# Softmax denominators of five more blocks through turning DMAs and GpSimd, in an attention and maxout kernel on one core

## The chip, the core and the metric

The kernel runs on one core of a Trainium2 chip. The metric is the device time of one execution, in microseconds (us). The core has a matrix engine (TensorE, shown as PE, its weight loads as PEld), a vector engine (VectorE, DVE), an activation engine (ScalarE, ACT), GpSimd (POOL) and SyncE (SP). Each takes its own instructions in a fixed order, and they wait for each other through semaphores. Transfers are issued from SP or from POOL and then run on the core's 16 DMA engines.

## The reference

An induced attention (32 learned points, 4 batches of 12544 rows of 128) is followed by a maxout layer without nonlinearity outside the maximum:

```
def mab(q, kv):
    s = scale * (q @ kv.transpose(0, 2, 1))
    s = s - s.max(-1, keepdims=True)
    a = np.exp(s)
    a /= a.sum(-1, keepdims=True) + 1e-09
    return a @ kv
h = mab(I, x)            # I: the 32 inducing points, for each batch
attn = mab(x, h)         # for each of 50176 rows: a softmax over 32
out = np.maximum(attn @ w1, attn @ w2) @ w_out     # d_ff 1024
```

In the second attention the denominator of a row is the sum of its 32 exponentials. The division by it is put off to the very end: the layer is linear but for the maximum, and a maximum commutes with a positive factor.

## The kernel before

**Tiling.** A batch is 98 chunks of 128 rows. Chunks are grouped into 28 blocks, seven for each batch, mostly 16 chunks in four "quarters" of four. A block's exponentials stand in one tile `e2` of 128 x 512: partition 32q+m holds inducing point m for quarter q, and the columns are rows of x. `stage` computes the scores of a block with four column-tiled matmuls (each uses a quarter of the array's columns) and `stage_exp` takes the exponential on ACT.

**The main loop.** For every block the kernel needs max(h1, h2) = h1 + relu(h2 - h1). A "phase" (`phase`, line 1093 of the profile) is four row-tiled matmuls that run beside each other, one for each quarter, into four PSUM banks. Each result of 128 x 512 is then put through a relu on ACT (line 1119) or DVE (line 1122). Between phases stand the "finals": 128 x 128 matmuls (`final_one`, line 907) that multiply those tiles by w_out into the bank of an output group (up to four chunks). The share of h1 is added by small matmuls of line 1093 with `m` (`L` jobs of a phase). `evict_group` (line 939) multiplies a finished group by the reciprocal of its denominators on DVE, and a DMA (line 969) issued from SP or POOL stores it. Output tiles `o` have six buffers.

**Denominators, first way.** `dens` multiplies each 128 x 128 piece of `e2` by `ones_q` (128 x 4) on TensorE: four sums for each row of x, one 128 x 4 matmul for each chunk column, up to two blocks in one call. Line 698 is the matmul, line 708 the reciprocal on DVE.

**Denominators, second way.** For blocks with `turned` set (the last batch, blocks 21 to 27) TensorE isn't used. `den_turn` issues a DMA that transposes `e2` from SP into a tile `eT` (line 717), `den_sum` adds up the 32 values on GpSimd in five halving additions (lines 727 and 729) in the space of `w1T`, and `den_rp` takes the reciprocal on DVE (line 736). The three are jobs in a list `pending`.

**The other transfers on SP.** x arrives by loads from POOL (line 166). For batches 1 to 3, `transpose_x_dma` turns it into `xT` with 14 transposing DMAs (line 172). `pool_scores` and `pool_turn` then make and turn the exponentials of the first attention (`eT`, line 378), and `pool_accum` sums them into h on TensorE (line 397). `den` and `eT` tiles come from one pool of buffers.

**What sets the order.** Every instruction stands in an order that is found when the program is built. `Clock` keeps an estimate of when TensorE, ACT, DVE and each PSUM bank are free. The loop at the end of the kernel asks it at every step whether to issue a phase, a final, or one of the side jobs for which `ready` says yes. `evict_relu` sends each relu to the engine that the estimate frees first. `DEV` is a table that overrides single decisions.

Of the kernel before, what the change touches and what calls it, by code (L numbers as in the profile page):

```python
# [16 lines left out]
INF = 1e9  # L17


class Clock:  # L20


    PAIR = 0.0558
# [4 lines left out]
    def __init__(self):  # L28
        self.pe = self.act = self.dve = 0.0
        self.mode = "full"  # L30
        self.bank = [0.0] * 8
        self.idle = {}
        self.log = []
        self.busy = {}
# [34 lines left out]
class Block:  # L69


    def __init__(self, quarters, full=()):
        self.quarters = quarters
        self.width = max(qu.w for qu in quarters if qu)
        self.b = [qu.b for qu in quarters if qu][0]
        self.staged = None
        self.rp = None
        self.units = []
        self.done = {}
        self.relu = {}  # L80
        self.last_group = {}
        self.groups = []
        for q, qu in enumerate(quarters):
            jobs = []
            t0 = 0
            for w in qu.subs if qu else []:
                for u in range(2 * w):
                    jobs.append((q, t0, w, u))
                t0 += w
            self.units.append(jobs)  # L90
            if qu:
                self.groups.append(Group(self, [(q, t) for t in range(qu.w)], q in full))
# [10 lines left out]
def kernel(  # L103
# [29 lines left out]
    rpp = ctx.enter_context(tc.tile_pool(name="rpp", bufs=5))  # L133
# [34 lines left out]
    def transpose_x_dma(b, j):  # L168
        i, h = divmod(j, 2)
        k0, n = parts[b][i]  # L170
        m = n // 2
        nc.sync.dma_start_transpose(
            xT_tiles[b % 2][:, k0 + m * h : k0 + m * (h + 1), :], xn_at[b, i][:, m * h : m * (h + 1), :]
        )
        st[b]["T", j] = ck.pe
# [21 lines left out]
    with tc.manual_schedule(engines={ET.PE, ET.DVE, ET.Activation, ET.Pool, ET.SP}):  # L197
# [128 lines left out]
        NEU = 5  # L326
        NU = K // U
# [7 lines left out]
        def pool_scores(b, u):  # L335
# [19 lines left out]
            ck.bank[bi] = ck.on_act(end, 0.65)  # L355
# [20 lines left out]
        def pool_turn(b, u):  # L376
            eT = etp.tile([128, 4, 128], F16, name=f"eT_{b}_{u}", tag="eT", bufs=NEU)
            nc.sync.dma_start_transpose(eT, st[b]["eu", u][0].rearrange("p (j t) -> p j t", j=4))
            st[b]["eT", u] = eT, ck.pe

        def pool_accum(b, u):
# [7 lines left out]
            if last:  # L389
                nc.vector.reduce_sum(out=acc[:, C : C + 1], in_=st[b]["es"], axis=AX.X)  # L390
                ck.on_dve(st[b]["eu", u][1], 0.1)
# [33 lines left out]
            end = ck.run(0.58 if last else 0.49, "col")  # L425
# [190 lines left out]

        for n, blk in enumerate(blocks):
            blk.turned = n > 20

        def stage(blk, now=True):  # L620
# [25 lines left out]
            end = ck.run(0.054 * wd, "col")  # L646
# [36 lines left out]
        def dens(blk):  # L683
# [23 lines left out]
            end = ck.run(0.029 * n)  # L707
            nc.vector.reciprocal(out=rp[:, 0:n, :].rearrange("p t q -> p (t q)"), in_=ps[:, 0 : 4 * n])
            ck.bank[bi] = ck.on_dve(end, 0.18 + 0.001 * 4 * n)
            for blk in blks:  # L710
                blk.rpr = ck.dve + 0.2

        def den_turn(blk):
# [3 lines left out]
            nc.sync.dma_start_transpose(eT, e2.rearrange("p (t k) -> p t k", k=128))  # L717
            blk.den = eT, ck.pe
            pending.append((den_sum, (blk,)))

        def den_sum(blk):
            wd = blk.width
            eT = blk.den[0].rearrange("p t (q m) -> p (t q) m", m=M)
            lo = 512 * (blk.index % 2)
# [5 lines left out]
            blk.dsum = acc[:, :, 0], ck.pe  # L730
            pending.append((den_rp, (blk,)))

        def den_rp(blk):
# [3 lines left out]
            ck.on_dve(ck.pe, 0.066 + 0.025 * wd)  # L737
# [187 lines left out]
        def evict_group(g, end):  # L925
# [40 lines left out]
            for b, c, s, m in runs:  # L966
                h = 2 if m == 4 and not by_pool and (gi in (56, 60, 64, 68, 72, 76) or 78 <= gi < 95) else m
                for lo in range(0, m, h):
                    queue.dma_start(out=outr[b, :, c + lo : c + lo + h, :], in_=osb[:, s + lo : s + lo + h, :])  # L969
# [24 lines left out]
        def want_linear():  # L994
# [113 lines left out]
        def evict_relu(q, a, u, bi, ps, end, eng=None):  # L1108
# [6 lines left out]
            ready = end + 0.03  # L1115
            if eng is None:
                eng = max(ck.act, ready) + 0.477 <= max(ck.dve, ready) + 0.597
            if eng:
                nc.scalar.activation(out=dst, in_=src, func=AF.Relu)  # L1119
                t = ck.on_act(ready, 0.477)  # L1120
            else:
                nc.vector.tensor_scalar(out=dst, in0=src, scalar1=0.0, scalar2=None, op0=ALU.max)  # L1122
                t = ck.on_dve(ready, 0.597)
# [36 lines left out]
        def ready(f, a):  # L1160

            now = ck.pe
            if f is den_turn:
                return a[0].staged <= now
            if f is den_sum:
                return a[0].den[1] + 7.5 <= now
            if f is den_rp:
                return a[0].dsum[1] + 3.0 <= now and a[0].index <= groups[min(state["g"], len(groups) - 1)].blk.index + 1
# [3 lines left out]
            if f is pool_turn and a[1] >= NEU and ("sum", a[1] - NEU) not in d:  # L1172
# [117 lines left out]
        while state["g"] < len(groups) or held:  # L1290
# [4 lines left out]
            if state["phase"] >= 3 and "m1" not in st[0] and w_of["w1out"] <= ck.pe and (ck.mode == "full" or final_ready() >= INF):  # L1295
# [71 lines left out]
```

## Time and profile before

| | |
|---|---|
| three runs | 324.11, 324.15, 324.23 us (median 324.15) |
| the profiled execution | 324.28 us, of which its span is 322.5 us |
| mean granted TensorE clock | 0.994 |
| line 698 on PE | 76 matmuls in 11 calls |
| line 736 on DVE | 7 reciprocals |
| HBM read and written | 27.54 MB and 25.69 MB |

The span runs from the first to the last instruction of the core; the times hold 1.78 us more in the profiled execution. Matmuls are pipelined: each has some 200 ns from its start to its end, while the next starts earlier, so the distance from start to start, not the busy time, says what one costs.

### The profile page before, as it was taken

To read this page: it belongs to the slowest core of one execution; us is meant where nothing else is said; L and a number is where in the kernel's file an instruction comes from. 1 tells how busy PE (TensorE), PEld (TensorE's weight loads), DVE (VectorE), ACT (ScalarE), POOL (GpSimd) and SP (SyncE) were. 2 spreads that over 40 slices of the span, in tenths; PEclk is the share of its full clock that TensorE was granted. 3 is DMA by queue.
4 is the path that set the end of the run, shared out by engine and by line. 5 is a ranking of instruction groups with operands and counts; after the bars stand their busy time and mean duration, and the time that the engine had idled before them with its cause. 6 is when DMAs were issued, how large, how long until landed. Compare 5 with 4: busy or idle time off the path is not lost.

```text
span 322.5 us, 12607 instructions
## 1 busy us (share of the span) xinstructions
PE 316.3 (98%) x5372; PEld 241.3 (75%) x5372; DVE 280.9 (87%) x506; ACT 281.6 (87%) x565; POOL 63.2 (20%) x136
## 2 busy tenths in 40 slices
PE   7999999999999999999999999999999999999996
PEld 3976777777777777777777777777777777777786
DVE  3369999899979998898999998989998999899973
ACT  4779899999978999989888999988969999999960
POOL 7472012212040121221040021222006400330000
PEclk9899999999999999999999999999999999999999
DMA  8999999974289999984269999963525322442233
GB/s 206 207 263 213 218 235 233 228 152 102 100 172 241 219 234 230 239 137 128 101 124 239 232 250 226 242 133 117 118 92 109 132 83 88 120 134 95 88 116 116
DMA packets 74072, 54.12 MB, mean 168 GB/s; under 512 B 56064, under 2 KB 64032, under 8 KB 74016
## 3 DMA queue, kind: packets, MB, share of 16 engines
q1 hardware_dynamic: 64320, 27.88, 40.7%
q0 software_dynamic: 9552, 25.37, 33.5%
q8 instruction: 42, 0.69, 0.9%
q14 instruction: 14, 0.11, 0.1%
q10 hardware_dynamic: 144, 0.07, 0.1%
HBM read 27.54 MB, written 25.69 MB: 165 GB/s over the span
## 4 chain that ended last, share of the span: by engine, by line
PE 92%; DMA 5%; ACT 1%; issue 1%; POOL 0%; DVE 0%; POOLq 0%
PE ps L907 62%; PE ps L1093 23%; DMA xn<-in_x_dram 5%; PE ps L637 2%; PE ps L397 2%; PE ps L341 1%; ACT relu L1119 1%; PE ps L698 1%; PE ps L531 0%; PE ps L236 0%; PE ps L315 0%; PE ps L442 0%; PE ps L266 0%; ACT hwd L504 0%; PE ps L489 0%
## 5 line engine op out<-in xcount | busy, mean ns | idle before, releaser
L1119 ACT ACTIVATE relu<-ps 128x512 f16<-128x512 f32 x462 | 244.0, 605 | 23.6 <-PE ps L1093 16.1
L1122 DVE TENSOR_SCALAR relu<-ps 128x512 f16<-128x512 f32 x322 | 206.5, 682 | 17.7 <-PE ps L1093 15.2
L907 PE MATMUL ps<-woutp,relu 128*128 128x128 f16 x3136 | 216.9, 220 | 0.1
L907 PEld LDWEIGHTS <-relu 128*128 128x128 f16 x3136 | 176.7, 98 | 38.7 <-issue 28.2
L1093 PE MATMUL ps<-e,hwd 32*128 32x512 f16 (+2 forms) x888 | 88.9, 358 | 0.6 <-ACT hwd L504 0.6
L969 POOL DMA_DIRECT2D out_dram<-o x44 | 23.8, 542 | 148.3 <-DVE o L939 134.1
L939 DVE TENSOR_TENSOR o<-ps,rp 128x512 f32<-128x512 f32 (+3 forms) x80 | 51.2, 639 | 1.6 <-PE ps L907 1.1
L1093 PEld LDWEIGHTS <-hwd 32*128 32x128 f16 x888 | 24.9, 91 | 22.1 <-issue 0.9
L1093 PE MATMUL ps<-m,e 32*128 32x128 f16 x381 | 38.9, 217 | 0.0
L1093 PEld LDWEIGHTS <-e 32*128 32x128 f16 x381 | 21.3, 92 | 2.9 <-issue 0.4
L939 DVE TENSOR_TENSOR o<-ps,rpt 128x512 f32<-128x512 f32 (+3 forms) x28 | 17.3, 619 | 4.2 <-PE ps L884 2.2
L166 POOL DMA_DIRECT2D xn<-in_x_dram x33 | 17.9, 556 | 6.4 <-DMA xn<-in_x_dram 4.5
L247 DVE COPY xT<-ps 128x768 f16<-128x768 f16 (+6 forms) x11 | 4.8, 459 | 8.7 <-PE ps L236 8.7
L352 ACT ACTIVATE eu<-ps 128x512 f16<-128x512 f32 x18 | 10.8, 616 | 0.0
L236 PE MATMUL ps<-identity,xn 128*128 128x128 f16 x98 | 9.5, 237 | 1.2 <-DVE inducingT L786 0.6
L656 ACT ACTIVATE e<-ps 128x512 f16<-128x512 f32 (+2 forms) x21 | 10.4, 584 | 0.0
L727 POOL TENSOR_TENSOR w1T<-den 128x256 f32<-128x256 f16 (+1 forms) x7 | 4.4, 630 | 26.7 <-DMA den<-e 26.7
L729 POOL TENSOR_TENSOR w1T<-w1T 128x64 f32<-128x64 f32 (+4 forms) x28 | 8.4, 300 | 2.2
L236 PEld LDWEIGHTS <-xn 128*128 128x128 f16 x98 | 6.7, 106 | 2.8 <-DVE xn L748 0.9
L250 ACT COPY xT<-ps 128x768 f16<-128x768 f16 (+5 forms) x10 | 6.4, 670 | 2.1 <-PE ps L236 2.0
L637 PE MATMUL ps<-xT,hT 128*32 128x512 f16 (+3 forms) x118 | 8.3, 355 | 0.0
L637 PEld LDWEIGHTS <-hT 128*32 128x32 f16 x118 | 3.2, 94 | 3.8 <-issue 2.1
(95 smaller groups left out, 115.1 us busy)
## 6 DMA issues: line engine op xcount, KB each, us to landing
out_dram<-o POOLq DMA_DIRECT2D x44, 256.0 KB, 3.8
xn<-in_x_dram POOLq DMA_DIRECT2D x24, 448.0 KB, 9.7
out_dram<-o SPq DMA_DIRECT2D x28, 256.0 KB, 2.7
out_dram<-o SPq DMA_DIRECT2D x46, 128.0 KB, 1.8
wf<-in_moe_w_dram POOLq DMA_DIRECT2D x4, 256.0 KB, 5.9
xn<-in_x_dram POOLq DMA_DIRECT2D x3, 224.0 KB, 8.8
xT<-xn SPq DMA_TRANSPOSE x42, 5.5
xf<-in_x_dram SPq DMA_DIRECT2D x1, 512.0 KB, 3.7
```

What stands on the lines that cost most here:

```text
L166: nc.gpsimd.dma_start(out=xn_at[b, i][lo:hi, 0:n, :], in_=xr[b, lo:hi, k0 : k0 + n, :])
L236: nc.tensor.transpose(ps[:, j, :], xn_at[0, i][:, g + j, :], identity16)
L352: nc.scalar.activation(out=eu, in_=ps, func=AF.Exp, scale=scale, accum_out=st[b]["es"][:, u : u + 1])
L637: nc.tensor.matmul(out=ps[32 * q : 32 * (q + 1), 128 * t : 128 * (t + n)], lhsT=hq, rhs=xT[:, c : c + n, :], start=True, stop=True, tile_p ...
L656: nc.scalar.activation(out=blk.e2[:, lo:hi], in_=ps[:, lo:hi], func=AF.Exp, scale=st[0]["rs"] if blk.b == 0 else scale,)
L729: nc.gpsimd.tensor_add(acc[:, :, 0:n], acc[:, :, 0:n], acc[:, :, n : 2 * n])
L907: nc.tensor.matmul(out=g.ps[:, 128 * c : 128 * (c + 1)], lhsT=g.blk.relu[q][:, 128 * (jb * w4 + t) : 128 * (jb * w4 + t + 1)], rhs=woutp[: ...
L939: nc.vector.tensor_mul(osb[:, 0:n, :], g.ps[:, 0 : n * C].rearrange("p (s c) -> p s c", s=n), rp)
L969: queue.dma_start(out=outr[b, :, c + lo : c + lo + h, :], in_=osb[:, s + lo : s + lo + h, :])
L1093: nc.tensor.matmul(**seq[i])
L1119: nc.scalar.activation(out=dst, in_=src, func=AF.Relu)
L1122: nc.vector.tensor_scalar(out=dst, in0=src, scalar1=0.0, scalar2=None, op0=ALU.max)
```

## The change

`TURNED` names twelve blocks in place of the last seven: 5, 10, 11, 12 and 19 are new. Their `dens` calls go, and `den_turn`, `den_sum` and `den_rp` come for each. The pool of `eT` has six buffers in place of five, that of the reciprocals nine in place of five. `Clock` gets estimates for SP, for POOL and for the time in which x is being loaded, and several of its costs are set anew. `ready` starts a turning only when no load runs by these estimates. Six more groups and three fewer whole ones are stored in halves, `small_m1(0)` may come one phase earlier, and `DEV` is another table.

```
-    PAIR = 0.0558
+    PAIR = 0.05595
...
+    def on_sp(self, ready, us, slow=0.0):
+        self.sp = max(self.sp, ready)
+        self.sp += slow if slow and self.sp < self.loads else us
+        return self.sp + (8.0 if self.sp < self.loads else 4.0)
...
-    rpp = ctx.enter_context(tc.tile_pool(name="rpp", bufs=5))
+    rpp = ctx.enter_context(tc.tile_pool(name="rpp", bufs=9))
...
+                ck.loads = ck.pe + 26.5
...
+        TURNED = (5, 10, 11, 12, 19, 21, 22, 23, 24, 25, 26, 27)
         for n, blk in enumerate(blocks):
-            blk.turned = n > 20
+            blk.turned = n in TURNED
...
         def den_turn(blk):
             uid[0] += 1
-            eT = etp.tile([128, 4, 128], F16, name=f"den_{uid[0]}", tag="eT", bufs=NEU)[:, 0 : blk.width, :]
+            eT = etp.tile([128, 4, 128], F16, name=f"den_{uid[0]}", tag="eT", bufs=NEU + 1)[:, 0 : blk.width, :]
             e2 = blk.e2[:, 0 : 128 * blk.width]
             nc.sync.dma_start_transpose(eT, e2.rearrange("p (t k) -> p t k", k=128))
-            blk.den = eT, ck.pe
+            eTs.append(lambda: blk.dsum is not None)
+            blk.den = eT, ck.on_sp(ck.pe, 1.3)
+            turned.append(blk)
             pending.append((den_sum, (blk,)))
...
-            lo = 512 * (blk.index % 2)
+            lo = 512 * (turned.index(blk) % 2)
...
-                h = 2 if m == 4 and not by_pool and (gi in (56, 60, 64, 68, 72, 76) or 78 <= gi < 95) else m
+                h = 2 if m == 4 and not by_pool and (70 <= gi < 77 and gi not in (74, 75) or 78 <= gi < 95) else m
...
         DEV = {
-            20000: 2, 50900: 2, 61200: 2, 91300: 1, 101300: 1, 111700: 1, 160800: 1, 210000: 3, 220000: 3,
...
+            20000: 2, 51000: 2, 61100: 2, 101200: 1, 101300: 1, 111700: 1, 141400: 1, 160000: 3, 161200: 1,
...
-                eng = max(ck.act, ready) + 0.477 <= max(ck.dve, ready) + 0.597
+                eng = max(ck.act, ready) + 0.487 <= max(ck.dve, ready_v) + 0.601
...
             if f is den_turn:
-                return a[0].staged <= now
+                if len(eTs) > NEU and not eTs[-NEU - 1]():
+                    return False
+                n = len(turned)
+                return a[0].staged <= now and ck.loads <= now and ck.sp <= now + (8.0 if a[0].b == 2 else 0.8) and (n < 3 or turned[n - 3].dsum is not None)
             if f is den_sum:
-                return a[0].den[1] + 7.5 <= now
+                n = turned.index(a[0])
+                return a[0].den[1] + 3.0 <= now and ck.pool <= now and (n < 2 or turned[n - 2].rp is not None)
             if f is den_rp:
-                return a[0].dsum[1] + 3.0 <= now and a[0].index <= groups[min(state["g"], len(groups) - 1)].blk.index + 1
+                return a[0].dsum[1] + 2.5 <= now
```

Counted over the whole built program, instructions change so: TensorE has 20 pairs of weight load and 128 x 4 matmul fewer (56 in place of 76) and otherwise the same matmuls, with as many changes between row-tiled, column-tiled and whole-array work (472) as before. Eleven relus move from DVE to ACT. DVE has two reciprocals of line 708 fewer and five of line 736 more. GpSimd has 25 additions more. SP issues five transposing DMAs and, through the other splitting, three stores more.

On SP this is the stretch in which the x of batch 2 is turned and its first attention runs; `xT` are the turned x, `eT` the turned exponentials of that attention, `o` the output tiles. Before:

```order
L172 DMA_TRANSPOSE xT_94<-xn_88 128x7x128 x2
L378 DMA_TRANSPOSE eT_0_3174<-eu_0_3130 128x4x128
L172 DMA_TRANSPOSE xT_94<-xn_89 128x7x128 x2
L172 DMA_TRANSPOSE xT_94<-xn_90 128x7x128
L378 DMA_TRANSPOSE eT_1_3361<-eu_1_3312 128x4x128
L172 DMA_TRANSPOSE xT_94<-xn_90 128x7x128
L378 DMA_TRANSPOSE eT_2_3487<-eu_2_3441 128x4x128
L378 DMA_TRANSPOSE eT_3_3517<-eu_3_3455 128x4x128
L378 DMA_TRANSPOSE eT_4_3802<-eu_4_3764 128x4x128
L378 DMA_TRANSPOSE eT_5_3831<-eu_5_3771 128x4x128
L969 DMA out_dram<-o_4012 128x512
```

With the change, `den_3122`, `den_3488` and `den_3593` being blocks 10, 11 and 12:

```order
L731 DMA_TRANSPOSE den_3122<-e_332_2341 128x4x128
L179 DMA_TRANSPOSE xT_94<-xn_88 128x7x128 x2
L387 DMA_TRANSPOSE eT_0_3201<-eu_0_3160 128x4x128
L179 DMA_TRANSPOSE xT_94<-xn_89 128x7x128
L387 DMA_TRANSPOSE eT_1_3255<-eu_1_3188 128x4x128
L179 DMA_TRANSPOSE xT_94<-xn_89 128x7x128
L179 DMA_TRANSPOSE xT_94<-xn_90 128x7x128 x2
L731 DMA_TRANSPOSE den_3488<-e_477_3167 128x4x128
L387 DMA_TRANSPOSE eT_2_3510<-eu_2_3467 128x4x128
L387 DMA_TRANSPOSE eT_3_3522<-eu_3_3474 128x4x128
L731 DMA_TRANSPOSE den_3593<-e_479_3174 128x4x128
L387 DMA_TRANSPOSE eT_4_3693<-eu_4_3665 128x4x128
```

Three of the five new turnings stand here: block 10's ahead of the last six pieces of x, block 11's right behind the last piece, and block 12's between the turnings of the first attention. None is moved past a store, but each `xT` and `eT` behind one of them is issued later by its time on SP.

On GpSimd the same stretch holds nothing but stores before; with the change the sums of blocks 11 and 12 stand between them (`w1T` is the space for the sums):

```order
L990 DMA out_dram<-o_3719 128x512
L743 TENSOR_TENSOR w1T<-den_3488 128x256
L745 TENSOR_TENSOR w1T<-w1T 128x16x8
L745 TENSOR_TENSOR w1T<-w1T 128x16x4
L745 TENSOR_TENSOR w1T<-w1T 128x16x2
L745 TENSOR_TENSOR w1T<-w1T 128x16
L990 DMA out_dram<-o_3786 128x512
L743 TENSOR_TENSOR w1T<-den_3593 128x256
```

The store of `o_3786` now comes after a sum that waits for a turning. Behind the four further additions of block 12 come two more stores and then the loads of x for the last batch.

On DVE the reciprocals of blocks 11 and 12 (`rpt_3928`, `rpt_4010`) come ahead of the output groups that need them:

```order
L440 TENSOR_TENSOR hacc_3626<-ps_3888,hacc_3626 128x128
L753 RECIPROCAL rpt_3928<-w1T 128x16
L1142 TENSOR_SCALAR relu_3688<-ps_3940 128x512
L956 TENSOR_TENSOR o_3965<-ps_3841,rpt_3477 128x512
L1142 TENSOR_SCALAR relu_3952<-ps_3969 128x512
L1142 TENSOR_SCALAR relu_3688<-ps_3998 128x512
L753 RECIPROCAL rpt_4010<-w1T 128x16
L1142 TENSOR_SCALAR relu_3952<-ps_4028 128x512
L1142 TENSOR_SCALAR relu_3746<-ps_4030 128x512
L956 TENSOR_TENSOR o_4041<-ps_3938,rpt_3928 128x512
```

Before, one reciprocal of line 708 for both blocks stood about there, behind a `dens` call on TensorE. Now each stands behind a sum on GpSimd, and the relus and output groups after it wait with it.

More of the change, by code (lines that the diff above doesn't have):

```diff
@@ L29, in __init__ @@
         self.pe = self.act = self.dve = 0.0
+        self.sp = self.pool = self.loads = 0.0
         self.mode = "full"
@@ L424, in pool_accum @@
                         )
-            end = ck.run(0.58 if last else 0.49, "col")
+            end = ck.run(0.54 if last else 0.445, "col")
             n = C + 1 if last else C
@@ L1171, in ready @@
                 return False
-            if f is pool_turn and a[1] >= NEU and ("sum", a[1] - NEU) not in d:
+            if f is pool_turn and len(eTs) > NEU and not eTs[-NEU - 1]():
                 return False
@@ L1294 @@
             side_work()
-            if state["phase"] >= 3 and "m1" not in st[0] and w_of["w1out"] <= ck.pe and (ck.mode == "full" or final_ready() >= INF):
+            if state["phase"] >= 2 and "m1" not in st[0] and w_of["w1out"] <= ck.pe and (ck.mode == "full" or final_ready() >= INF):
                 small_m1(0)
```

34 lines of the change are left out of this document (22 added, 12 removed), and 5 rows, old and new, of the table DEV.

## The prediction

> **What bounds the kernel now.** I read the page's shares first, then its chain of waits, then the busy time by stretches, then what TensorE waited for.
>
> ```profile
> span 322.5 us, 12607 instructions
> PE 316.3 (98%) x5372; PEld 241.3 (75%) x5372; DVE 280.9 (87%) x506; ACT 281.6 (87%) x565; POOL 63.2 (20%) x136
> ...
> PE 92%; DMA 5%; ACT 1%; issue 1%; POOL 0%; DVE 0%; POOLq 0%
> ```
>
> ```profile
> 0.00:30.00 30.00, 26.68 (x453) 19.71 (x454) 15.99 (x43) 21.46 (x46) 17.68 (x37) 0.94 1.06 223
> 30.00:80.00 50.00, 50.00 (x857) 37.62 (x855) 46.35 (x79) 47.20 (x98) 6.55 (x13) 1.00 1.00 198
> ...
> 120.00:160.00 40.00, 40.00 (x694) 30.12 (x693) 36.87 (x64) 36.76 (x79) 5.94 (x11) 1.00 0.80 169
> ...
> 240.00:280.00 40.00, 40.00 (x647) 30.26 (x644) 36.98 (x67) 37.26 (x73) 9.27 (x25) 1.00 0.36 103
> ```
>
> ```profile
> PE ps L753 <- DVE warm L217: 1.2, 1, 1.2
> ...
> PE ps L1093 <- ACT hwd L504: 0.6, 1, 0.6
> ```
>
> The three fences are the page, the busy time by stretches (columns PE, PEld, DVE, ACT, POOL, granted clock, DMA share, GB/s) and TensorE's waits. TensorE holds 92% of the chain, it is never idle from 30 to 280 us, and its waits are all from the ramp. DVE and ACT are at some 93% in the middle. A busy PE may still hide short delays, since matmuls overlap, so I look at distances from start to start:
>
> ```profile
> 76.31 1.08 PE L397 MATMUL ps<-xn,eT 128*32 128x128 f16 x64
> 77.32 0.50 PE L1093 MATMUL ps<-e,hwd 32*128 32x512 f16 x4
> 77.75 0.95 PE L907 MATMUL ps<-woutp,relu 128*128 128x128 f16 x14
> 78.64 0.40 PE L1093 MATMUL ps<-e,hwd 32*128 32x512 f16 x4
> 78.97 0.23 PE L907 MATMUL ps<-woutp,relu 128*128 128x128 f16 x1
> ...
> 84.81 0.51 PE L1093 MATMUL ps<-e,hwd 32*128 32x256 f16 x5
> 85.26 0.90 PE L907 MATMUL ps<-woutp,relu 128*128 128x128 f16 x13
> ```
>
> The phase at 78.64 takes 0.33 us until the finals behind it start. The one at 77.32 takes 0.43: it waited 0.10 us for PSUM banks, after a long run of line 397. The one at 84.81 takes 0.45. Compared in the same way, the 218 phases behave like the one at 78.64 nearly throughout: after 30 us five exceed it by over 0.03 us, these two and three of 0.03 to 0.05, some 0.3 us together. In the ramp there is more:
>
> ```profile
> 27.78 0.39 PE L1093 MATMUL ps<-e,hwd 32*128 32x512 f16 x1
> ...
> 28.50 0.23 PE L907 MATMUL ps<-woutp,relu 128*128 128x128 f16 x1
> ```
>
> The phase at 27.78 takes 0.72 us, 0.39 too many. The change leaves the order here as it is up to the first final behind it. So the time is what TensorE has to do, and only what is taken from TensorE, or makes it wait, counts.
>
> **What comes off TensorE.** Twenty pairs of weight load and 128 x 4 matmul go, four for each of five blocks.
>
> ```profile
> 152.07 0.51 PE L907 MATMUL ps<-woutp,relu 128*128 128x128 f16 x6
> 152.42 0.34 PE L698 MATMUL ps<-ones_q,e 128*128 128x4 f16 x8
> 152.62 0.78 PE L907 MATMUL ps<-woutp,relu 128*128 128x128 f16 x11
> ```
>
> This is the call for blocks 11 and 12, which goes entirely. Eight pairs take 152.62 - 152.42 = 0.20 us, 25 ns each; their own 0.34 us overlaps the next finals. Ahead of it, six finals take 0.35 us, where six at 56 ns (fourteen in 78.64 - 77.75 = 0.89 us, less a tenth for the change of mode) would take 0.34: an edge of about 0.01 us for each of the two calls that go (11 become 9). Sum: 20 x 0.025 + 2 x 0.01 = **0.52 us**. Nothing else on TensorE changes its number, and changes of mode are as many as before, so I cost the new grouping of the column-tiled runs at nothing; whichever pieces stand together, each is paid once.
>
> The Trainium skill speaks for more. TensorE: Matmul & The Clock Gate, section "Back-to-back issue gap", says that in a stream of weight loads and matmuls the distance is set by both and gives some 81 ns for a pair with 128 columns. By it the sum would be 20 x 0.081 = 1.6 us. The trace disagrees here: 25 ns for these pairs and some 56 ns for the finals.
>
> **What is added, and what hides it.** The five turnings cost what the seven do now:
>
> ```profile
> L717 SPq DMA_TRANSPOSE den<-e x7: 1191/1217/1994, 242.5 to 280.0; - x7
> ...
> DMA to landing us min/median/max: 2.4/3.5/4.4
> ```
>
> ```profile
> L378 SPq DMA_TRANSPOSE eT<-eu x18: 1190/1218/2346, 61.9 to 224.7; - x18
> ...
> DMA to landing us min/median/max: 2.4/3.5/5.2
> ```
>
> ```profile
> L172 SPq DMA_TRANSPOSE xT<-xn x42: 1220/1740/5557, 33.6 to 208.8; - x42
> ...
> DMA to landing us min/median/max: 3.0/5.5/10.6
> ```
>
> ```profile
> 245.03 0.66 POOL L727 TENSOR_TENSOR w1T<-den 128x256 f32<-128x256 f16 x1 [0.79 <-DMA den<-e]
> 245.77 1.47 POOL L729 TENSOR_TENSOR w1T<-w1T 128x128 f32<-128x128 f32 x4
> 247.19 0.66 POOL L727 TENSOR_TENSOR w1T<-den 128x256 f32<-128x256 f16 x1
> ```
>
> Each holds SP for 1.2 us (median) and lands after 3.5. The new ones stand between the turnings of x and of the first attention, so their bounds are the rows of those: 2.4 to 10.6 us. I take 3.5 to 5.2, the row of `eT`, which have the same shape and place. A sum takes 247.19 - 245.03 = 2.2 us on GpSimd, which is 20% busy. On TensorE's path all this costs nothing as long as the sum is there when DVE comes to the reciprocal. How much cover is there? For blocks 11 and 12:
>
> ```profile
> 135.42 1.78 SPq L172 DMA_TRANSPOSE xT<-xn  x1
> 137.29 12.79 SPq L378 DMA_TRANSPOSE eT<-eu  x4
> ```
>
> ```profile
> 153.39 0.68 DVE L939 TENSOR_TENSOR o<-ps,rp 128x512 f32<-128x512 f32 x1
> 153.99 0.35 DVE L708 RECIPROCAL rp<-ps 128x32 f32<-128x32 f32 x1
> ```
>
> Block 11's turning follows the last piece of x, so it can start at about 137.3. With 5.2 us to land and 2.2 to be summed it is ready by 144.7. DVE reaches the reciprocal of line 708 at 153.99 before; the new one stands one output group earlier, some 3 us, so at about 151. The cover is some 6 us. Block 12 starts behind block 11 and two turnings of `eT`, 3 x 1.3 us later, and has its reciprocal five DVE instructions (some 3 us) later: some 5 us. The stores behind the sums on GpSimd wait 2.2 us longer each:
>
> ```profile
> out_dram<-o POOLq DMA_DIRECT2D x44, 256.0 KB, 3.8
> ```
>
> They land after 3.8 us. The 108 output groups come at (319 - 29)/108 = 2.7 us, so that with six buffers an output tile has some 16 us for its store; 2.2 more cost nothing. Were a cover gone, DVE would stand still with all relus behind the reciprocal and their banks would stay full. TensorE would then wait for all of it but some 1.3 us, my estimate from one phase with its finals (78.64 - 77.32), which it can still work through.
>
> GpSimd could slow DVE down, since 5 x 2.2 us more of its work run beside it:
>
> ```profile
> L1122 DVE TENSOR_SCALAR relu<-ps 128x512 f16<-128x512 f32 x11 | 7.2, 685 | 0.2
> ```
>
> ```profile
> L1122 DVE TENSOR_SCALAR relu<-ps 128x512 f16<-128x512 f32 x322 | 206.5, 682 | 17.7 <-PE ps L1093 15.2 <-PE ps L907 0.5 <-ACT relu L1119 0.4
> ```
>
> The first row is DVE from 245 to 254.6 us, where four sums run nearly without a gap: 685 ns against 682 over all. Nothing. Nor did DVE wait for any of the seven sums so far, the last number being its idle time ahead of them:
>
> ```profile
> L736 DVE RECIPROCAL rpt<-w1T 128x16 f32<-128x16 f32 (+1 forms) x7 | 1.7, 236 | 0.0
> ```
>
> **The shift to ACT.** Eleven relus move.
>
> ```profile
> L1119 ACT ACTIVATE relu<-ps 128x512 f16<-128x512 f32 x462 | 244.0, 605 | 23.6 <-PE ps L1093 16.1
> ```
>
> ACT gets 11 x 0.605 = 6.7 us, 288.3 of 322 us or 89%; DVE loses 11 x 0.682 = 7.5 us and gains some 0.5 net in reciprocals. Both still wait for TensorE (23.6 and 17.7 us of idle time), so I cost it at nothing. Bounds: a gain of the 0.3 us of short waits counted above, if the new order has none; a loss of the same size, if its long column-tiled runs (in batch 1 all six turned tiles are summed in one run, where it was two) make waits like the 0.10 us at 77.32, three or four of them.
>
> **Sum.** 324.28 - 0.52 = 323.76 for the profiled execution, which stands 0.13 above the median of the runs; against the median 324.15 - 0.52 = 323.63. I predict **323.6 us**.
>
> **The rivals.**
> *The short waits go as well.* A newly found order with better estimates could remove the 0.3 us after 30 us and some 0.1 of the ramp: 324.15 - 0.52 - 0.4 = 323.2. For it: those waits stand at places that the new table reaches. Against: they are small and scattered, and a new order makes its own. A pair costing its weight load is a part of this case: at the 96 ns that a weight load lasts, 20 pairs would be 1.9 us and the time 322.2. Against that stands 152.42 to 152.62; I give it 2 in 100.
>
> ```profile
> L698 PEld LDWEIGHTS <-e x76: 94/96/99, 27.2 to 239.5; 128*128 128x128 f16 x76
> ```
>
> The sentence of the skill quoted above would put it at 322.5, in between.
>
> *A turned denominator is late (the other side).* Place: the reciprocals of blocks 11 and 12 on DVE. If a turning lands like the slowest piece of x (10.6 us, against 5.2) and starts two slow issues later (5.557 us at most, say 4 more in all), it is 5.4 + 4 = 9.4 us late against 5 to 6 of cover. DVE stands 3.4 to 4.4 us; less 1.3 in the banks, some 2.6 reach TensorE, once. Time: 323.6 + 2.6 = 326.2. It decides from 7.5 us of delay (5 + 1.3 + 1.2), where 323.6 + 1.2 = 324.8 is over 0.2% slower. For it: the turnings of x do stretch that far, and from 120 to 160 us the DMA engines are still 80% busy. Against: the turnings of `eT` in the same stretch, also on SP, landed within 5.2 us, and DVE never waited for a sum.
>
> *ACT or the banks bind.* The 11 relus and longer runs cost 0.1 us each at four or five places more: 324.1.
>
> **How the numbers follow.** Forecast 46%, with its own range 323.3 to 323.95 (0.52 with 0.3 to either side); short waits gone 26% with the weight load in it; late 14%; ACT or banks 14%. 0.2%, about what a measurement of this kernel tells from no change, is 0.65 us: faster means under 323.50. That takes a quarter of the forecast (11%) and nearly all of the short waits (24%): 35%. Slower means over 324.80: most of the late case and a little of the last, 14%. The rest, 51%, is within. The range goes from 323.1 to 324.6.
>
> **What would show it.** Line 698 with 56 matmuls, at 25 ns from start to start. Phases at 0.33 us as before; the sum of what exceeds it says which of the first, second and fourth cases it is. No idle time of DVE ahead of line 753 (the new line of `rpt`), and `den` landing within 5.2 us. PE idle after 30 us, or DVE waiting for GpSimd, makes the prediction wrong, and so does a time under 323.1, which would mean that the pairs cost more than the 25 ns that I read.

## The result, and the profile after

The changed kernel took 324.73 us in the median of 19 runs (323.82 to 325.11), the kernel before beside it 324.20 us (324.04 to 324.48): a ratio of 1.0014, 95% interval 1.0008 to 1.0020. It is 0.5 us slower where 0.5 us less was predicted: a small loss, but the interval excludes no change. Its runs spread over 1.3 us, those before over 0.4. The profiled execution of the changed kernel, 323.82 us, is the fastest of its 19, so its span flatters it.

The page and TensorE's list of groups first (busy time, share, instructions):

```profile
span 322.1 us, 12608 instructions
PE 315.3 (98%) x5352; PEld 239.9 (74%) x5352; DVE 276.5 (86%) x498; ACT 285.5 (89%) x576; POOL 73.2 (23%) x161
...
PE 92%; DMA 5%; ACT 1%; issue 1%; POOL 0%; DVE 0%; POOLq 0%
...
L1139 ACT ACTIVATE relu<-ps 128x512 f16<-128x512 f32 x473 | 247.8, 607 | 21.0 <-PE ps L1113 16.3
L1142 DVE TENSOR_SCALAR relu<-ps 128x512 f16<-128x512 f32 x311 | 202.0, 684 | 19.1 <-PE ps L1113 16.7
```

```profile
L710 PE MATMUL ps<-ones_q,e 128*128 128x4 f16 x56 | 2.7, 165 | 0.0
```

Twenty matmuls fewer, 11 relus moved, the chain as before: all of that came as predicted. So the time has to be taken apart by place. Three marks do it: the start of the first final matmul (end of the ramp), the start of the last matmul, and the end of the span. TensorE's rows in order of time (start, us, engine, line, operation), before:

```profile
25.79 0.27 PE L907 MATMUL ps<-woutp,relu 128*128 128x128 f16 x2
...
319.40 0.22 PE L884 MATMUL ps<-m1bd,e 128*128 128x128 f16 x1
```

and after:

```profile
25.56 0.27 PE L924 MATMUL ps<-woutp,relu 128*128 128x128 f16 x2
...
318.77 0.22 PE L901 MATMUL ps<-m1bd,e 128*128 128x128 f16 x1
```

The stretch between the two marks, called the body from here on, is 293.6 us before and 293.2 after: 0.4 us shorter. What follows the last matmul, called the tail, is 322.5 - 319.4 = 3.1 us before and 3.3 after, and in three other executions of the changed kernel 3.6 to 3.8. The loss is there. In the tail the last group is divided on DVE, and its store (issued by ScalarE) and the three ahead of it (issued by SyncE) land. Those four stores, from issue to landing, before:

```profile
DMA to landing us min/median/max: 1.6/1.8/2.3
```

and after:

```profile
DMA to landing us min/median/max: 1.8/2.2/3.4
```

They are issued 2.0 and 0.7 us ahead of the start of the last matmul and 0.2 and 0.6 us behind it, in both kernels alike, and are of 512, 384, 256 and 128 columns. The longest landing is that of the first. What is in its way stands in the DMA view of the moments around its issue (317.37 us before, 316.73 after); each fence has the packets of all queues that start in a short window. Before, 317.15 to 317.45:

```profile
q8 instruction: 1, 0.02, 19.7%
out_dram<-o SPq DMA_DIRECT2D x1, 256.0 KB, 2.3
```

After, 317.65 to 317.85, and then 318.4 to 318.9:

```profile
q1 hardware_dynamic: 41, 0.08, 107.2%
q8 instruction: 1, 0.02, 38.6%
```

```profile
DMA packets 0, 0.00 MB, mean 0 GB/s; under 512 B 0, under 2 KB 0, under 8 KB 0
```

A packet of queue q8, the one that brings instructions, starts 0.16 us ahead of the store's issue before (at 317.21, for 0.95 us) and 0.95 us behind it after (at 317.68, for 1.24 us), when the store's own packets have just begun to move. The page counts 42 such packets of 0.69 MB in all, so 16 KB each. By the packet records, 120 of the 128 packets of that store had started by 318.29; the other eight, one sixteenth, which is one DMA engine's part, start one behind the other from 318.92, the moment at which the 16 KB are through. That engine stays late for the three stores behind: the one with 384 columns lands in 2.5 instead of 1.8 us. (The Trainium skill, DMA: Bandwidth & Descriptors, section "Queues, rings and completion order", has each engine take turns between its queues by whole packets; these records agree.)

Why does the packet come later? Counted from its start to the end of the span, TensorE still has this to do, before:

```profile
L907 PE MATMUL ps<-woutp,relu 128*128 128x128 f16 x38 | 2.6, 219 | 0.0
L884 PE MATMUL ps<-m1bd,e 128*128 128x128 f16 x6 | 0.8, 219 | 0.0
```

and after:

```profile
L924 PE MATMUL ps<-woutp,relu 128*128 128x128 f16 x21 | 1.4, 219 | 0.0
L901 PE MATMUL ps<-m1bd,e 128*128 128x128 f16 x3 | 0.5, 219 | 0.0
```

44 matmuls before, 24 after (those already running are counted; 40 and 20 start behind it). The difference is the twenty matmuls that the change took out: the packets stand at places in TensorE's list of instructions, one for every 127 matmuls on average (100 to 171 between single packets in the trace of after), and the list became 40 instructions shorter ahead of the end. (Runtime: NRT & Kernel Launch of the Trainium skill, section "Instruction fetch mechanics", gives blocks of 16 KiB, 256 instructions, fetched by a DMA queue of the sequencer's own; the 42 packets for some 10,700 instructions agree.)

That was a reading of one trace. It became the theory FETCH below only after the first experiments had taken away the others.

### The profile page after: what moved, and what is told of

Read it like the earlier page. It is cut to its first block, busy times and chain, and to the rows that moved or that the text cites. A ratio compares the mean times of both kernels' runs of the same rounds, so it can differ in the third digit from the quotient of the medians.

```text
span 322.1 us, 12608 instructions
## 1 busy us (share of the span) xinstructions
PE 315.3 (98%) x5352; PEld 239.9 (74%) x5352; DVE 276.5 (86%) x498; ACT 285.5 (89%) x576; POOL 73.2 (23%) x161
## 4 chain that ended last, share of the span: by engine, by line
PE 92%; DMA 5%; ACT 1%; issue 1%; POOL 0%; DVE 0%; POOLq 0%
PE ps L924 62%; PE ps L1113 23%; DMA xn<-in_x_dram 5%; PE ps L649 2%; PE ps L407 2%; PE ps L349 1%; ACT relu L1139 1%; PE ps L542 0%; PE ps L710 0%; PE ps L243 0%; PE ps L453 0%; PE ps L322 0%; PE ps L273 0%; ACT hwd L515 0%; PE ps L901 0%
## 5 line engine op out<-in xcount | busy, mean ns | idle before, releaser
L1139 ACT ACTIVATE relu<-ps 128x512 f16<-128x512 f32 x473 | 247.8, 607 | 21.0 <-PE ps L1113 16.3
L1142 DVE TENSOR_SCALAR relu<-ps 128x512 f16<-128x512 f32 x311 | 202.0, 684 | 19.1 <-PE ps L1113 16.7
L956 DVE TENSOR_TENSOR o<-ps,rp 128x512 f32<-128x512 f32 (+3 forms) x60 | 37.5, 626 | 1.7 <-PE ps L924 1.5
L956 DVE TENSOR_TENSOR o<-ps,rpt 128x512 f32<-128x512 f32 (+3 forms) x48 | 30.9, 644 | 5.4 <-PE ps L924 3.6
L745 POOL TENSOR_TENSOR w1T<-w1T 128x64 f32<-128x64 f32 (+4 forms) x48 | 14.6, 304 | 3.8
L743 POOL TENSOR_TENSOR w1T<-den 128x256 f32<-128x256 f16 (+1 forms) x12 | 7.8, 649 | 31.3 <-DMA den<-e 16.4
L243 PE MATMUL ps<-identity,xn 128*128 128x128 f16 x98 | 8.7, 220 | 1.6 <-DMA xn<-in_x_dram 1.2
L243 PEld LDWEIGHTS <-xn 128*128 128x128 f16 x98 | 6.0, 97 | 3.4 <-DMA xn<-in_x_dram 1.9
```

What stands on the lines that cost most here:

```text
L243: nc.tensor.transpose(ps[:, j, :], xn_at[0, i][:, g + j, :], identity16)
L745: nc.gpsimd.tensor_add(acc[:, :, 0:n], acc[:, :, 0:n], acc[:, :, n : 2 * n])
L956: nc.vector.tensor_mul(osb[:, 0:n, :], g.ps[:, 0 : n * C].rearrange("p (s c) -> p s c", s=n), rp)
```

## The experiments

All 16 experiments, with the marks of each profiled execution (us) and, in the first two rows, the two kernels themselves; "packet" is the number of matmuls that start behind the start of the last q8 packet. The times are medians; "before" is the kernel before run beside it on the same chip.

| run | first final | body | packet | tail | time | before |
|---|---|---|---|---|---|---|
| before | 25.79 | 293.62 | 40 | 3.10 | | 324.20 |
| after | 25.56 | 293.21 | 20 | 3.28 | 324.73 | 324.20 |
| e1_again | 25.76 | 293.23 | 18 | 3.65 | 324.42 (one) | 324.22 |
| e2_no_new | 25.93 | 293.23 | 18 | 4.54 | 324.98 | 324.22 |
| e3_no_new_dma | 25.75 | 293.24 | 19 | 4.26 | 325.30 | 324.22 |
| e4_order_only | 25.68 | 293.85 | 36 | 3.42 | 324.85 | 324.22 |
| f1_after_fetch20 | 27.64 | 293.79 | 40 | 3.09 | 326.84 | 325.47 |
| f2_after_fetch40 | 26.41 | 293.22 | 55 | 3.10 | 325.04 | 325.47 |
| f3_before_fetch20 | 26.39 | 293.62 | 60 | 3.09 | 326.83 | 325.47 |
| f4_before_fetch_late | 26.83 | 293.61 | 5 | 3.48 | 326.20 | 325.47 |
| g1_after_gap20 | 27.21 | 294.19 | 38 | 3.09 | 326.06 | 324.28 |
| g2_after_gap40 | 27.71 | 293.22 | 57 | 3.08 | 326.17 | 324.28 |
| g3_before_gap20 | 26.44 | 293.61 | 50 | 3.09 | 324.94 | 324.28 |
| g4_after_control | 25.79 | 293.23 | 3 | 3.58 | 324.53 | 324.28 |
| h1_after_fill4 | 26.04 | 293.23 | 36 | 3.10 | 323.90 | 324.30 |
| h2_after_fill5 | 25.72 | 293.24 | 42 | 3.09 | 323.91 | 324.30 |
| h3_before_fill4 | 25.84 | 293.61 | 54 | 3.09 | 324.27 | 324.30 |
| h4_after_control | 25.82 | 293.22 | 19 | 3.83 | 324.65 | 324.30 |

### Is it the new chains, or the new order?

**e1_again**: the changed kernel unchanged, for a second profiled execution.

> The changed kernel, unchanged, for a second profile: its executions lie between 323.8 and 325.1 us, and the one profile so far is of the shortest. If the spread comes from turned denominators that land late (theory one), an execution over 324.4 us shows DVE idle ahead of line 753 or GpSimd waiting for den tiles over 5 us, at one of the blocks 5, 10, 11, 12 or 19. If it comes from the new order (theory two), DVE never waits there, and phases of line 1113 that take 0.4 us and more in place of 0.33 add up to 0.6 us more than in the first profile.

**e2_no_new**: the five new turnings and sums are left out; their reciprocals read a tile of ones, so those blocks' denominators are missing from the output.

```
+        NEW = (5, 10, 11, 12, 19)
...
+            if blk.index not in NEW:
                 nc.gpsimd.tensor_add(acc, eT[:, :, 0 : M // 2], eT[:, :, M // 2 : M])
...
+            src = ones32[:, 0 : 4 * wd] if blk.index in NEW else blk.dsum[0]
```

> The changed kernel's order with the five new turnings and sums left out; the reciprocals of blocks 5, 10, 11, 12 and 19 read a constant, so their rows of the output are not divided. Theory one (the new chain is late in some executions, or its transfers slow others): 323.6 to 323.8 us, all executions within 0.4 us of each other, some 0.9 us under the changed kernel. Theory two (the new order makes its own waits): no change against the changed kernel, 324.5 to 324.9 us and a spread of 1 us.

**e3_no_new_dma**: only the five turning DMAs are left out; GpSimd adds up `e2` as it stands, so that the denominators of those blocks are sums over other values.

```
+            if blk.index in NEW:
+                eT = e2.rearrange("p (t k) -> p t k", k=128)
+            else:
...
                 nc.sync.dma_start_transpose(eT, e2.rearrange("p (t k) -> p t k", k=128))
```

> The five new turning DMAs left out, the GpSimd sums kept: they add up the exponentials as they stand, so the denominators of these blocks are wrong. If the transfers are what costs: as without the whole chain, 323.6 to 323.8 us. If the sums on GpSimd do (their place ahead of stores and loads): still 324.5 us or more. Theory two: 324.5 to 324.9 us as well, then told apart by the run without the whole chain.

**e4_order_only**: the old seven blocks turned, with the new estimates, table and buffers.

```
-        TURNED = (5, 10, 11, 12, 19, 21, 22, 23, 24, 25, 26, 27)
+        TURNED = (21, 22, 23, 24, 25, 26, 27)
```

> The changed planner with its costs and its table, but only blocks 21 to 27 turned, as before: the five blocks are summed on TensorE again, and the order is found for that. Theory one: 324.15 to 324.4 us (the time of before) with a small spread of 0.4 us. Theory two: over 324.7 us, with a spread of 1 us, since the new costs alone make the order tighter.

Without the chains the kernel is no faster: ratio 1.0020 (1.0011 to 1.0029) without turnings and sums, 1.0027 (1.0016 to 1.0038) without the turnings alone. So neither a late denominator nor the added DMAs and GpSimd sums cost the 0.5 us. The body is 293.2 us in all of e1 to e3, to within 0.03, so nothing in it depends on the chains, and the longer phases of theory two would show in it as well. Both theories of these expectations fall, though the time that theory two gave came true in e4 and nearly in e2. What varies is the tail, and e2 and e3 have the longest. The four last stores in e2:

```profile
DMA to landing us min/median/max: 2.4/3.2/4.3
```

e4 (1.0017, 1.0008 to 1.0026) is slower by another road: its body is 0.23 us longer than before, and its tail 0.32, though its stores land in 1.6 to 2.5 us. SyncE's records at the end show where the tail comes from. Behind the last store SyncE waits for the semaphores of the transfers one after another, some 60 ns each, and in e2, e3 and e4 five or six more of these waits than in the kernel before stand behind the one that ends last. From the last landing to the end of the span it takes 1.30, 1.22 and 1.22 us in these three, 0.92 to 0.98 in the 15 other traces. Without that the tail is 3.1 us in e4, and 4.2 and 4.0 in e2 and e3. e4 has the packet at 36 and its runs spread over 0.33 us only, against 1.29 for the changed kernel.

### Does the tail follow the packet?

FETCH says that the packet's place in TensorE's list makes the tail; QUEUE says that the new order's load on SyncE's queue does. f1 to f3 put instructions in at the very start and so move the packet alone; f4 gives the kernel before so many that the packet comes later there.

```
-        for _ in range(WARM):
-            nc.tensor.matmul(out=ps, lhsT=warm[:, 0:128], rhs=warm, start=True, stop=True)
+        for _ in range(29):
+            nc.tensor.matmul(out=ps[:, 0:156], lhsT=warm[:, 0:128], rhs=warm[:, 0:156], start=True, stop=True)
```

(f2: 49 of 92 columns; f4: 117 of 38.)

> The changed kernel with its 9 warm-up matmuls of 128x512 at the very start of TensorE replaced by 29 of 128x156: about the same columns, but 20 matmuls and 20 weight loads (40 TensorE instructions) more ahead of everything else, and nothing else moved. Theory FETCH: the 16 KB packets of the instruction queue q8 come at fixed places in TensorE's instruction list; the change took 20 matmuls with their 20 weight loads out, so the last such packet came 1.09 us before the last matmul's start instead of 2.19 us, 0.95 us behind the issue of the first of the last four stores (3.42 us to its landing) instead of 0.16 us ahead of it (2.26 us). With the 40 instructions given back the packet stands 2.2 us ahead of the last matmul again, that store lands in 2.0 to 2.3 us, the span ends 3.1 us behind the start of the last matmul (3.28 to 4.5 in the runs so far), and the body's gain of 0.4 us is seen: 323.8 us. Theory QUEUE: the last stores are late because of what the new order puts on the queue of SyncE ahead of them; that is untouched, so the time stays at 324.7 us with the tail at 3.3 to 4.5 us.

> As the run before, with 49 warm-up matmuls of 128x92 in place of the 9 of 128x512, so 80 TensorE instructions more. FETCH: the last 16 KB packet stands 3.3 us ahead of the last matmul's start, a microsecond before the first of the last four stores is issued; all four land in their undisturbed 2.0, 1.8, 1.7 and 1.6 us, the tail is 3.0 us and the time 323.7 us, spread over the runs by some 0.3 us where the changed kernel spread over 1.3. QUEUE: 324.7 us as the changed kernel.

> The kernel before with 29 warm-up matmuls of 128x156 in place of its 9 of 128x512. FETCH: its last 16 KB packet moves from 2.2 to 3.3 us ahead of the last matmul and off the last stores altogether; the first of them lands in 1.97 instead of 2.26 us, and the time is 324.0 to 324.2 us, so 0.0 to 0.2 below the kernel before. QUEUE: 324.2 us, no change. The two hardly differ here; the run says what the warm-up edit itself costs, and whether the changed kernel gains against a kernel before that has the packet out of the way as well (FETCH: 0.3 to 0.4 us between this run and the one before).

> The kernel before with 117 warm-up matmuls of 128x38 in place of its 9 of 128x512: 216 TensorE instructions more, which is 40 less than the 256 that a 16 KB packet holds at 64 bytes each (an estimate from 42 packets for 10,700 instructions). FETCH: the last packet therefore comes 1.1 us before the last matmul, where it stands in the changed kernel, though nothing of the change is in it: the first of the last stores takes 3.4 us or more to land, the tail grows from 3.1 to between 3.3 and 4.5 us, and the time by 0.2 to 1.4 us, about 325 us in the median. QUEUE: the tail stays at 3.1 us and the time at 324.2 us. Should the warm-up take longer in this form, the start of the first final matmul shows it and is taken off.

The tail did what FETCH said: 3.09 and 3.10 us with the packet at 40 and 55, with SyncE's list of transfers unchanged, and 3.48 in the kernel before with the packet at 5 (it was meant to be at 20; its place varies, see g4 below). QUEUE has no room for that. In f4 the packet came too late for the first store, which landed in 2.2 us and not in the 3.4 that were expected. Late were the second (2.7 us) and the third, whose issue held SyncE for 0.80 us in place of 0.33:

```profile
L969 SPq DMA_DIRECT2D out_dram<-o x3: 332/332/802, 318.4 to 320.6; - x3
```

The third store's issue is as long, 0.44 to 0.97 us, in all profiled executions whose packet is still under way then (e1 to e3, f4, g4, h4). The size of the tail follows the packet as well. In the five executions with the packet at 18 to 20 (after, e1, h4, e3, e2) it is through 0.15, 0.40, 0.47, 0.56 and 0.81 us behind the start of the last matmul, and the tail, less the longer closing waits of e2 and e3, is 3.28, 3.65, 3.83, 3.97 and 4.17 us.

The time didn't follow. The kernel before itself went from 324.26 to 328.04 us on that chip, so these medians bear little, but the first final matmul came 0.6 to 2 us late in all four.

g1 to g3 therefore leave the warm-up alone and use a wait of the ramp (g2: 26 there and 14 in an earlier one); g4 is the changed kernel beside them.

```
+            for _ in range({(3, 0): 20}.get((i, piece), 0)):
+                nc.tensor.transpose(ps[:, 0, 0:32], warm[0:32, 0:128], identity16[0:32, 0:32])
             for j in range(m):
```

> The changed kernel with 20 transposes of 32x32 (idle zeros, into the bank that is overwritten next) ahead of the fourth block's transposes in the loading ramp, where the changed kernel's TensorE waited 0.90 us for the DMA of xn: 40 TensorE instructions more, warm-up and everything else as in the changed kernel. FETCH: the last 16 KB packet stands some 2.2 us ahead of the last matmul's start, tail 3.1 us, body 293.2 us from the first final matmul to the last: span and time 0.4 us below the kernel before run beside it (323.8 us on a quiet chip). QUEUE: 0.5 us above the kernel before, as the changed kernel.

> As the run before with 40 such transposes, 26 there and 14 ahead of the second block's: 80 TensorE instructions more. FETCH: the last packet stands 3.3 us ahead of the last matmul, clear of the last four stores (1.97, 1.8, 1.7, 1.6 us), tail 3.1 us, body 293.2 us; 0.4 us below the kernel before, by up to 0.2 more where the ramp hides the transposes worse or better. QUEUE: 0.5 us above the kernel before.

> The kernel before with the same 20 transposes in the ramp. FETCH: its packet goes from 2.2 to 3.3 us ahead of the last matmul; the tail stays at 3.1 us, since the last of the stores was undisturbed already, and the time stays within 0.2 us of the kernel before. Between this and the changed kernel with 20: 0.4 us in favour of the changed one, all in the body (293.6 against 293.2 us). QUEUE: no change from the kernel before either.

> The changed kernel unchanged, on the same chip as the three runs above. Both theories: about 0.5 us above the kernel before; FETCH adds that its profile shows the last 16 KB packet 0.9 to 1.1 us behind the issue of the first of the last four stores, that store's landing over 3 us, and a tail of 3.3 to 4.5 us.

Again tails of 3.08 and 3.09 us, again a late ramp, and now beside a quiet kernel before: ratios of 1.0049 (1.0030 to 1.0068), 1.0057 (1.0044 to 1.0070) and 1.0032 (1.0017 to 1.0047). My expectation of the time was wrong in all three. The reason stands in TensorE's rows in order of time. Before:

```profile
20.51 0.33 PE L315 MATMUL ps<-et,xn 128*128 128x32 f16 x7
20.69 0.21 PE L298 MATMUL ps<-ones,et 128*128 128x1 f16 x2
```

and in g3, which has twenty small matmuls more ahead of the same place:

```profile
20.49 0.33 PE L317 MATMUL ps<-et,xn 128*128 128x32 f16 x7
21.32 0.22 PE L300 MATMUL ps<-ones,et 128*128 128x1 f16 x2 [0.50 <-issue]
```

The next matmul starts 0.18 us behind the seven before, 0.83 in g3, and what it waited for is no semaphore ("issue"). In all four runs with twenty more (f1, f3, g1, g3) this wait stands in front of the 351st matmul of the trace, and in no other run. By the packet records a q8 packet is under way from 18.9 to 19.9 us there. In this stretch TensorE takes a pair every 25 ns, over twice as fast as the finals, so I read it as TensorE having come to the end of the instructions that it had. The place fits, and so does the moment: in the four the 351st matmul starts 1.35 to 1.43 us behind the end of that packet, and in none of the 18 traces earlier than 1.35 us behind it. No record shows it directly. What f2, f4 and g2 lost in the ramp isn't this, and its cause is open. In f1 and g1 the granted clock fell as well, to 0.57 and 0.63 in the stretch from 22 to 30 us. From the first final matmul to the 21st they take 4.45 and 4.84 us, where the changed kernel takes 3.88; that is all that their bodies lost. The stretch in f1 (columns as in the prediction):

```profile
22.00:30.00 8.00, 7.65 (x81) 4.34 (x82) 5.53 (x12) 6.44 (x14) 3.99 (x7) 0.57 1.16 208
```

g4 also shows that the packet's place isn't exact: at 3 matmuls from the end in this execution of the same program, where three others had 18 to 20. Its first store landed in 2.2 us, against the over 3 of its expectation, and its tail of 3.58 came as in f4.

### The packet moved behind the ramp

h1 splits six filling matmuls at 26 to 28 us, which are there to be thrown away, in four each, h2 in five; h3 does to the kernel before what h1 does, and h4 is the changed kernel.

```
-            for _ in range(n):
+            for _ in range(4 * n):
                 nc.tensor.matmul(
-                    out=g.ps[:, 0:256],
+                    out=g.ps[:, 0:64],
                     lhsT=warm[:, 0:128],
-                    rhs=warm[:, 0:256],
+                    rhs=warm[:, 0:64],
```

> The four runs with instructions added in the loading ramp had the last packet where FETCH wanted it and a tail of 3.09 us, but lost 0.6 to 2 us in the ramp: 20 matmuls more ahead of it put a wait of 0.68 to 0.98 us, which no semaphore ends, in front of matmul 350, in the stretch where TensorE goes through 128x32 and 128x1 matmuls at 25 ns each (not there without them). So here the instructions go in behind the ramp: each of the six filling matmuls of 128x256 (line 881, at 26.1 to 27.6 us) becomes four of 128x64, with the same columns; 18 matmuls and 18 weight loads more, everything else as in the changed kernel. FETCH: no such wait in the ramp, first final matmul at 25.6 to 25.8 us as in the changed kernel, body 293.2 us (at most 0.1 more), last packet some 38 matmuls ahead of the last, tail 3.1 us: 0.3 to 0.45 us below the kernel before beside it, 323.8 us on a quiet chip, so the fastest of all. If the tail is not what the change lost: 0.2 to 0.6 us above the kernel before, as the changed kernel.

> As the run before, each filling matmul in five of 128x51: 24 matmuls and 24 weight loads more. FETCH: last packet some 43 matmuls ahead of the last, the first of the last stores in 2.0 to 2.4 us, tail 3.1 us, the ramp's end 0.0 to 0.1 us later than with four: 0.25 to 0.45 us below the kernel before. Otherwise 0.2 to 0.6 us above it.

> The kernel before with its six filling matmuls in four of 128x64 each. FETCH: its last packet goes from 40 to 58 matmuls ahead of the last; tail 3.1 us as before, body 293.6 us, time within 0.15 us of the kernel before. That says what the edit costs by itself, and h1 stands 0.3 to 0.45 us below this run.

> The changed kernel unchanged, beside the three. 0.2 to 0.6 us above the kernel before, tail 3.3 to 4.5 us, its spread over the runs over 1 us where h1's is under 0.6.

In time, body and tail all four came out as FETCH had them; h1's first final matmul, at 26.04 us, was 0.2 us later than expected, and h4's runs spread over 0.99 us where over 1 was expected. h1 took 323.90 us (323.81 to 324.15), ratio 0.9985 (0.9976 to 0.9994); h2 323.91, ratio 0.9984 (0.9975 to 0.9993); h3 324.27, ratio 0.9999 (0.9991 to 1.0008); h4 324.65 (324.31 to 325.30), ratio 1.0010 (1.0001 to 1.0019). The marks and the stores of h1:

```profile
26.04 0.27 PE L924 MATMUL ps<-woutp,relu 128*128 128x128 f16 x2
...
319.27 0.22 PE L901 MATMUL ps<-m1bd,e 128*128 128x128 f16 x1
```

```profile
DMA to landing us min/median/max: 1.6/1.8/2.6
```

and the stores of h4, where the packet starts 1.0 us behind the issue of the first of them:

```profile
DMA to landing us min/median/max: 2.3/2.8/4.0
```

The books close: h4 less h1 is 0.75 us in the medians, and 3.83 - 3.10 = 0.73 in the tails; h3 less h1 is 0.37, and 293.61 - 293.23 = 0.38 in the bodies. The profiled execution of h1, 324.15 us, is its slowest, with a late ramp; h2's is its median, and there h4 less h2 is 0.74 in the medians and 3.83 - 3.09 = 0.74 in the tails. h1, with 18 matmuls more than the changed kernel, is faster than both kernels.

## Why the prediction was wrong

**The step that failed** is the last sentence of what bounds the kernel: "So the time is what TensorE has to do, and only what is taken from TensorE, or makes it wait, counts." The sum took 0.52 us off the whole time and held the tail behind the last matmul to be fixed. It isn't: taking 40 instructions from TensorE moved its last instruction packet from 0.16 us ahead of the first of the last four stores to 0.95 us behind its issue, and the tail grew by 0.2 to 0.7 us in the four profiled executions of the changed kernel (after, e1, g4 and h4, packet at 3 to 20), in three of them by more than the 0.4 that the body gained. Taking the packet off the stores (h1, h2) gives the predicted direction and 0.4 us of the predicted 0.52. The median of the 19 runs, 324.73, would by the same sum need a tail of some 4.0 us (an estimate: 3.10 + 0.41 + 0.53, the ramp as before); the longest profiled one of this kernel is 3.83. No rival had it either, and none of the prediction's signs could have shown it: all look at the body. The clue was in the trace of before, among the stores that were counted but not looked at one by one.

**The mechanism in the body was right, its size a little off.** The term of 0.52 us measured 0.38 to 0.41 (h3 against h1, before against after). Eight pairs at line 710 still take 0.21 us from start to start, 26 ns each:

```profile
114.87 0.34 PE L710 MATMUL ps<-ones_q,e 128*128 128x4 f16 x8
115.08 0.44 PE L924 MATMUL ps<-woutp,relu 128*128 128x128 f16 x5
```

So the price holds, and short waits explain the missing 0.1 and more: behind 30 us, what the phases of over 0.34 us exceed 0.33 us by adds up to 0.61 us in the trace of after and 0.40 before, 0.2 more, as the prediction's bound for the new order had it in kind ("make waits like the 0.10 us at 77.32"). The rival in which the short waits go (323.2 us) falls with this. That these waits come from the new order fits e4, whose body grew by 0.23 with the twenty pairs still in and is 0.6 longer than the changed kernel's; its order isn't quite that of the changed kernel, though, so this is not shown.

**The chains cost nothing**, as predicted. The reciprocals of line 753 and their idle time, and the turnings' landing:

```profile
L753 DVE RECIPROCAL rpt<-w1T 128x16 f32<-128x16 f32 (+1 forms) x12 | 2.9, 240 | 0.0
```

```profile
DMA to landing us min/median/max: 2.3/2.6/5.0
```

5.0 us at most against the 5.2 taken. DVE's relu takes 684 ns against 682. The rival of a late denominator fell with this and with e2. **The eleven relus on ACT** cost nothing that shows, though no run tells whether a part of those 0.2 us of short waits is theirs: over the seven stretches from 30 to 318 us, TensorE is busy without a gap in the sum of the busy times.

```profile
sum 288.00, PE 288.00 PEld 220.23 DVE 259.66 ACT 263.92 POOL 55.21; mean PE 41.14 PEld 31.46 DVE 37.09 ACT 37.70 POOL 7.89
```

**The rival of the weight load's price** (322.2 us) fell too, and with it the 81 ns a pair of the Trainium skill's TensorE: Matmul & The Clock Gate, section "Back-to-back issue gap": with the tail out of the way the change is worth 0.4 us, not 1.6. That figure is for 128 columns, and the pairs here have 4; the finals, which have 128, take 56 ns in these traces.

## What to carry to other kernels

Split a time into ramp, body and tail before a small gain is believed: half a microsecond in 320 is no more than one disturbed store at the end. An edit that adds or removes instructions can also move later instruction fetches, on a queue that no source line names (here twenty pairs moved the last one by twenty matmuls), so look at where the last one stands against the last stores, and move it by splitting or merging matmuls that are there only to fill. Where the body gains and the time doesn't, compare the landing times of single stores, not their medians by line.

## What the runs showed of the hardware that was not expected

A 16 KB instruction packet takes 0.9 to 2.1 us in these 18 traces, and a store that meets it waits with a sixteenth of its packets. In the trace of after, the store of 256 columns issued at 309.66 us, 1.2 us ahead of such a packet, landed so, and one like it at 313.28, without any, so:

```profile
DMA to landing us min/median/max: 3.9/3.9/3.9
```

```profile
DMA to landing us min/median/max: 1.7/1.7/1.7
```

In the body that costs nothing: it takes 293.21 to 293.24 us in all ten executions of the changed kernel's order without the lower clock of f1 and g1. At the end the span waits for it. The second thing is the wait of 0.7 to 1.0 us in the ramp, in front of the 351st matmul, that twenty small matmuls placed ahead of it brought about, and its cause named above is a reading, not a proof. The third is that the same program had its last packet 18 to 20 matmuls from the end in three executions and 3 in another; why is open, and so is why the third store's issue alone is held. Of the 0.25 and 0.57 us by which the medians of e2 and e3 lie above the changed kernel's, the closing waits account for 0.37 and 0.29; what is left of e3's is open.
